# One step of an attention and two expert layers: other order at the start, at the hand-over and in the late steps

## The chip, the cores and the metric

The kernel runs on one core of one Trainium2 chip. The metric is the device time of one execution in microseconds. PE is the matrix engine (TensorE), ACT the scalar engine, DVE the vector engine, POOL GpSimd, and SP the queue that issues most transfers.

## The reference

```python
def _attn_ref(q, k, v, g_norm):                # 4 batches, 8 heads, 576 tokens, 64 wide
    kv = np.einsum('bhsd,bhse->bhde', k, v)
    out = np.einsum('bhsd,bhde->bhse', q, kv)
    rms = np.sqrt(np.mean(out * out, axis=-1, keepdims=True) + 1e-06)
    return (out / rms * g_norm).astype(np.float32)

def _moe_ref(x, domain_probs, w1, w2):         # N=2304, D=512, E=4, F=1024
    p = domain_probs / (domain_probs.sum(-1, keepdims=True) + 1e-09)
    for e in range(E):
        h = np.maximum(x @ w1[e], 0.0)
        out += p[:, e:e + 1] * (h @ w2[e])

def _moe2_ref(x, expert_emb, tau, w1, w2):     # 8 experts, one for each token
    logits = xn @ en.T / tau                   # xn, en: rows divided by their norms
    expert_idx = np.argmax(logits, axis=1)
    gate_w = probs[np.arange(N), expert_idx]   # softmax of the logits
    for e in range(E):
        h = np.maximum(x[mask] @ w1[e], 0.0)
        out[mask] = gate_w[mask, None] * (h @ w2[e])
```

The output of the first becomes x of the second, and its output x of the third.

## The kernel before

The 2304 tokens are 18 tiles of 128, and six units of 384 (three tiles). Each fp32 product of the two expert layers is made of three products of a high part and a low part (split, L60): ACT casts the high part, DVE, or POOL where it is named, subtracts it to get the low part. Instructions run on each engine in the order in which the code issues them, since the schedule is written by hand.

The opening (from L1061): for each of four batches, k and v of two heads give a 64 x 64 product each (kv_unit, L149), copied to a block-diagonal tile kv_bd. For batches 0 and 1 the 576 tokens lie as 72 partitions of 8 rows each (RW = 8), so one unit has 8 steps for two heads, 16 products; for batches 2 and 3 they lie as 128 partitions of 4 rows and a rest of 64 rows, 5 steps, 10 products. In the trace each product of this kind counts as two matrix instructions. Batch 0 uses the tile of the second layer's embeddings (en_b) and the four raw weight buffers; batch 1 uses en_b, two other spare tiles, and for its last pair two raw weight buffers later (last_kv, L1185). The q tiles 0 to 2 are issued by ACT. The first unit's tiles are transposed, multiplied with kv_bd, normalised and transposed again (q_first, x_first, xt_unit); later tiles go through qt_unit, x_unit, x_norm and xt_unit, which are spread over the steps of the expert phases by times in the phase (spread, run_steps, att). An item with time t is issued after the first step whose summed time reaches t. heat() issues filler products.

The first expert layer has phases (p, e, fh): pair of units, expert, half of F. The first four phases run one unit plainly (plain_phase: four products of P1T / 4 each, six second-layer steps), the others a Strassen scheme for two units with 14 + 12 steps (strassen_steps, l2_steps, run_steps at L1240). The raw weight stream has four buffers (issue, take); expert 0's split weights go to DRAM and come back later (hold, fetch).

When a tile of the second layer's input is ready, its logits come by DVE from a reload (logits_v, eight reductions, tiles 0 to 11) or by PE (logits_t, logits_u, tiles 12 to 17). logits_v, route_a and route_b are generators in a list bg; background(n), called after each step, takes up to n pieces from the list and runs what is due at this tick. route_a places the first 12 tiles into NA = 5 jobs of 128 tokens for one expert, route_b the rest into up to 20 jobs. run_steps has the pace n of each step: every second step for the first two pairs of units, every step for the last pair.

The routed jobs (period, full_period, from L1303): period(s) makes the first layer of job s in two halves (m1_unit, line 1267), calls mid1 after each quarter, then the second layer of job s - 1 (m2_unit, line 1289) with mid2 between its quarters, in which the next job's x is transposed and split (ahead_of, tx_unit), and the transposes of h (th_unit). mid1 and mid2 call side(), which issues one weight split from a list (slot_split) and then background(). Job 0 has no second layer beside it; its w2 splits stand in work2, so they are issued after period(0). The placing products are line 513, in invert().

Of the kernel before, what the change touches and what calls it, by code (L numbers as in the profile page):

```python
# [8 lines left out]
F32 = mybir.dt.float32  # L9
# [11 lines left out]
def attn_moe_moe_kernel(ctx: ExitStack, tc: tile.TileContext, q, k, v, g_norm, dprobs, w1, w2, emb, tau, w1b, w2b, out):  # L21
# [98 lines left out]
    RW = 8  # L120
    SR = S // RW

    RL = 2 * RW * DH
    kv_at = {}

    def raw_home():
        return rawp.tile([128, 2 * D], F32, name="raw", tag="raw")

    def kv_homes(b):
        flat = en_b.rearrange("p e n -> p (e n)")  # L130
        part = [flat[:, RL * i:RL * i + RL] for i in range(4)]
        if b == 0:
            homes = part + [raw_home() for _ in range(4)]
        else:
            spare = sum_p.tile([128, 4, 2, 128], F32, name="wsum", tag="wsum").rearrange("p a b c -> p (a b c)")
            homes = [xr[:, 1].rearrange("p c n -> p (c n)"), spare] + part
        for pair in range(len(homes) // 2):
            kv_at[b, pair] = homes[2 * pair:2 * pair + 2]

    def kv_rows(b, pair, o):  # L140
        return kv_at[b, pair][o][0:SR, 0:RL]

    def load_kv_rows(b, pair):
        for o, src in enumerate((k, v)):
            nc.sync.dma_start(
                out=kv_rows(b, pair, o).rearrange("p (h x) -> p h x", h=2),
                in_=src[b, 2 * pair:2 * pair + 2].rearrange("h (p r) d -> p h (r d)", r=RW),
            )

    def kv_unit(b, pair, tag="kv"):  # L150
        ps = psp.tile([128, DH], F32, name="pskv", tag=tag)
        if b < 2:
            kr, vr = (kv_rows(b, pair, o).rearrange("p (h r d) -> p h r d", h=2, d=DH) for o in range(2))
            for c in range(RW):
                for i in range(2):
                    nc.tensor.matmul(out=ps[64 * i:64 * i + 64], lhsT=kr[:, i, c], rhs=vr[:, i, c], start=(c == 0), stop=(c == RW - 1))
        else:
# [11 lines left out]
        if b >= 2:  # L169
            issue()  # L170
# [1228 lines left out]
```

## Time and profile before

| | |
|---|---|
| three runs | 1150.51 us median (1149.87 to 1150.71) |
| the profiled execution | 1150.26 us |
| its span, first to last instruction | 1148.5 us |
| busy PE, DVE, ACT, POOL | 1114.1, 633.1, 486.3, 191.2 us |
| first expert product | 32.95 us after the span's start |
| first Strassen phase | starts near 113 us |
| first product of a routed job | 849.21 us |

The page shows busy time of each engine, the granted clock, transfers and the costliest groups. A timeline row reads: start, duration, engine, line, operation, output<-inputs, count, and in brackets the time for which the engine stood idle before it and what ended that. A busy PE is not PE at full speed: at the lower clock the same product takes longer.

### The profile page before, as it was taken

What the parts mean: (1) busy time and instruction counts of PE and PEld (TensorE: products, weight loads), DVE (VectorE), ACT (ScalarE), POOL (GpSimd) and SP (SyncE); (2) the same over time, 40 slices, a digit from 0 to 9 for tenths busy, and PEclk for the clock granted to TensorE, in tenths of its full rate; (3) what the DMA queues carried; (4) which work ended last, traced back from release to release, by engine and by line L of the source; (5) the groups of instructions that cost most, each with busy time, mean ns of one, the idle gap of its engine ahead of it and who ended that gap; (6) DMA issues with size and microseconds to landing.
All of it is one profiled execution on the core that took longest, in us unless ns stands there. A gap on an engine that the chain in (4) does not pass through costs nothing. (4 is left out here: it accounts for less than half of the span.)

```text
span 1148.5 us, 17340 instructions
## 1 busy us (share of the span) xinstructions
PE 1114.1 (97%) x5982; PEld 974.7 (85%) x5982; DVE 633.1 (55%) x1187; ACT 486.3 (42%) x892; POOL 191.2 (17%) x232
## 2 busy tenths in 40 slices
PE   8899999999999999999999999999997899999997
PEld 8788998888888988899988888999886788888886
DVE  1655664567784556543565684333458674366362
ACT  2534545544454222233333222222456475476462
POOL 1211331223341000100120001000010111211211
PEclk7999999999999999999999999999998899999999
DMA  8664878667777455455464544555454593575571
GB/s 207 180 221 166 311 257 299 236 244 283 284 246 282 166 214 179 170 201 202 174 226 169 220 170 179 200 202 202 171 195 166 184 329 109 172 273 205 168 250 41
DMA packets 87044, 239.87 MB, mean 209 GB/s; under 512 B 17109, under 2 KB 32469, under 8 KB 86816
## 3 DMA queue, kind: packets, MB, share of 16 engines
q1 hardware_dynamic: 76384, 213.44, 52.4%
q0 software_dynamic: 7440, 24.41, 6.2%
q10 hardware_dynamic: 3120, 0.79, 0.4%
q8 instruction: 50, 0.82, 0.3%
q14 instruction: 50, 0.41, 0.1%
HBM read 230.22 MB, written 56.63 MB: 250 GB/s over the span
## 5 line engine op out<-in xcount | busy, mean ns | idle before, releaser
L976 PE MATMUL bank<-w2h,hh 128*128 128x512 f32 x576 | 227.9, 396 | 2.0 <-ACT hh L853 1.9
L976 PE MATMUL bank<-w2l,hh 128*128 128x512 f32 x576 | 225.2, 391 | 0.9 <-DVE w2l L62 0.8
L976 PE MATMUL bank<-w2h,hl 128*128 128x512 f32 x576 | 225.4, 391 | 0.5 <-DVE hl L856 0.5
L881 PE MATMUL bank<-xth,w1h 128*128 128x384 f32 x616 | 160.4, 341 | 4.0 <-ACT s L888 1.4
L881 PE MATMUL bank<-xtl,w1h 128*128 128x384 f32 x616 | 156.8, 335 | 0.0
L881 PE MATMUL bank<-xth,w1l 128*128 128x384 f32 x616 | 156.7, 335 | 0.0
L985 DVE SCALAR_TENSOR_TENSOR acc<-bank,dp,acc 128x512 f32<-128x512 f32 x120 | 89.8, 749 | 110.3 <-PE bank L976 110.1
L976 PEld LDWEIGHTS bank<-w2h,hl 128*128 128x128 f32 x576 | 108.2, 188 | 25.4 <-DVE hl L856 2.4
L976 PEld LDWEIGHTS bank<-w2h,hh 128*128 128x128 f32 x576 | 108.2, 188 | 25.3 <-ACT hh L853 4.0
L976 PEld LDWEIGHTS bank<-w2l,hh 128*128 128x128 f32 x576 | 108.2, 188 | 22.4 <-DVE w2l L62 1.1
L881 PEld LDWEIGHTS bank<-xth,w1h 128*128 128x128 f32 x616 | 109.2, 188 | 9.8 <-ACT s L888 2.2
L881 PEld LDWEIGHTS bank<-xtl,w1h 128*128 128x128 f32 x616 | 111.4, 188 | 0.0
L881 PEld LDWEIGHTS bank<-xth,w1l 128*128 128x128 f32 x616 | 111.3, 188 | 0.0
L62 DVE TENSOR_TENSOR w2l<-raw,w2h 128x1024 fp32r<-128x1024 f32 x64 | 76.5, 1221 | 58.7 <-ACT w2h L61 55.1
L892 POOL TENSOR_TENSOR sv<-sv,s 128x384 f32<-128x384 f32 x44 | 48.8, 1110 | 353.0 <-ACT sv L888 301.3
L888 ACT COPY s<-bank 128x384 f32<-128x384 f32 x88 | 42.3, 481 | 143.7 <-PE bank L881 143.7
L370 DVE CUSTOM_DVE_ANT_0 scr<-row,en_b 128x512 bf16<-128x512 f32 x96 | 68.8, 717 | 17.4 <-DMA row<-x1d 12.6
L1289 PE MATMUL psy<-w2h,hth 128*128 128x512 f32 x176 | 71.6, 407 | 0.4 <-ACT hth L1280 0.4
L1289 PE MATMUL psy<-w2l,hth 128*128 128x512 f32 x176 | 69.5, 395 | 0.0
L1289 PE MATMUL psy<-w2h,htl 128*128 128x512 f32 x176 | 69.2, 393 | 0.0
L61 ACT CAST w2h<-raw 128x1024 fp32r<-128x1024 f32 x64 | 65.5, 1054 | 5.5 <-DMA raw<-in_moe_w_dram 2.1
L62 DVE TENSOR_TENSOR w1l<-raw,w1h 128x256 fp32r<-128x256 f32 (+2 forms) x75 | 55.5, 757 | 19.6 <-ACT w1h L61 19.2
(251 smaller groups left out, 1670.2 us busy)
## 6 DMA issues: line engine op xcount, KB each, us to landing
raw<-in_moe_w_dram SPq DMA_DIRECT2D x224, 512.0 KB
w1h<-held_w SPq DMA_DIRECT2D x28, 896.0 KB
w1l<-held_w SPq DMA_DIRECT2D x28, 896.0 KB
w2h<-held_w SPq DMA_DIRECT2D x34, 512.0 KB
w2l<-held_w SPq DMA_DIRECT2D x34, 512.0 KB
held_w<-w1h SPq DMA_DIRECT2D x16, 896.0 KB
held_w<-w1l SPq DMA_DIRECT2D x16, 896.0 KB
held_w<-w2h SPq DMA_DIRECT2D x16, 512.0 KB
```

The source lines that it names most:

```text
L61: nc.scalar.copy(hi, raw)
L62: (eng or nc.vector).tensor_tensor(out=lo, in0=raw, in1=hi.bitcast(F32), op=ALU.subtract)
L370: nc.vector.tensor_tensor_reduce(out=scr, in0=x, in1=en_b[:, e], scale=1.0, scalar=0.0, op0=ALU.mult, op1=ALU.add, accum_out=lg[:, t, e:e + 1]
L881: nc.tensor.matmul(out=ps, lhsT=wform(wo, b, w)[:, c], rhs=xform(xo, x)[:, c], start=start and n == 0, stop=(n == 5), skip_group_check=True)
L888: nc.scalar.copy(t, src)
L892: (eng or nc.vector).tensor_tensor(out=out, in0=a, in1=b, op=ALU.add)
L976: nc.tensor.matmul(out=ps, lhsT=h_t[o][f][u][:, ns], rhs=w[j][:, a], start=(k == 0 and m == 0), stop=(k == 3 and m == 2))
L985: nc.vector.scalar_tensor_tensor(out=fin, in0=ps, scalar=dp[:, t, e:e + 1], in1=ac, op0=ALU.mult, op1=ALU.add)
L1289: nc.tensor.matmul(out=ps, lhsT=x[:, f], rhs=w[j][:, o], start=(f == 0 and i == 0), stop=(f == NF - 1 and i == 2))
```

## The change

k and v of batches 0 and 1 now also lie as 128 partitions of 4 rows and a rest of 64 rows: batch 0 comes through the raw weight stream, batch 1 into en_b with its rest in a spare tile; the separate last pair is gone. q tiles 0 to 2 are issued by SP behind batch 0. The k/v units of batch 0 share one PSUM buffer and are not mixed with q transposes. The next loads follow as buffers come free. All three direct w1 parts of the first block are split before batch 1's units. In the first two phases the attention steps have times of their own, and w2's splits start at 0 instead of 1. Tile 8's steps are spread over 12 to 28 instead of 17 to 31.1 in their phase. In the last pair of units, experts 0 and 1 have the pace of every second step. The last tile's logits come one tick sooner, and the squares are issued after the copy of the transposes, into another tile. The gate is cut in three: inverse norms ahead of the choice of the expert, the exponential after it, the sum after the places. In period(0) the w2 splits of job 0 stand in the list that mid1 uses.

```diff
-    def load_tail(b):
-        t = kv_p.tile([S - MAIN, 2, H, DH], F32, name="kvtail", tag="tail", bufs=1)
+    def load_tail(b, home=None):
+        t = home if home is not None else kv_p.tile([S - MAIN, 2, H, DH], F32, name="kvtail", tag="tail", bufs=1)
...
     def kv_unit(b, pair, tag="kv"):
+        early = b == 1
+        r = en_b[:, 2 * pair:2 * pair + 2].rearrange("p i n -> p (i n)") if early else take("kv", b, pair)
+        r = r.rearrange("p (i h r d) -> p i h r d", i=2, h=2, d=DH)
+        tl = tail_raw[b]
         ps = psp.tile([128, DH], F32, name="pskv", tag=tag)
-        if b < 2:
-            kr, vr = (kv_rows(b, pair, o).rearrange("p (h r d) -> p h r d", h=2, d=DH) for o in range(2))
-            for c in range(RW):
-                for i in range(2):
-                    nc.tensor.matmul(out=ps[64 * i:64 * i + 64], lhsT=kr[:, i, c], rhs=vr[:, i, c], start=(c == 0), stop=(c == RW - 1))
...
     def logits_t(t, x):
         xx = late["tmp"].tile([128, NC, 128], F32, name="xx", tag="xx")
-        due.append((tick[0] + 2, t, lambda: logits_u(t, xx)))
-        nc.scalar.activation(out=xx.rearrange("p c n -> p (c n)"), in_=x, func=ACTF.Square, accum_out=ssq[:, t:t + 1])
+        due.append((tick[0] + (2 if t < NT - 1 else 1), t, lambda: logits_u(t, xx)))
         ps = psp.tile([128, NC, 128], F32, name="pslt", tag=f"x{t % 2}" if t < NT - 1 else nxt("l2"))
         for c in range(NC):
             nc.tensor.transpose(ps[:, c], x[:, 128 * c:128 * c + 128], ident)
         nc.scalar.copy(xx, ps)
+        sq = late["tmp"].tile([128, R, 128], BF16, name="po", tag="po", bufs=2)
+        nc.scalar.activation(out=sq.rearrange("p r n -> p (r n)"), in_=x, func=ACTF.Square, accum_out=ssq[:, t:t + 1])
...
-    def gates(t0, t1, tag):
...
-        rx = inv_norm(ssq[:, s], [128, T], tag)
-        yield 0
-        tt(l, l, bc(rx, sh, 2), ALU.mult)
-        nc.scalar.activation(out=l, in_=l, func=ACTF.Exp)
-        yield 1
-        nc.vector.tensor_reduce(out=sm, in_=l, axis=AX.X, op=ALU.add)
+    def gate_exp(t0, t1, rx):
+        l = lg[:, t0:t1]
+        tt(l, l, bc(rx, [128, t1 - t0, E2], 2), ALU.mult)
+        nc.scalar.activation(out=l, in_=l, func=ACTF.Exp)
+
+    def gate_sum(t0, t1):
+        s = slice(t0, t1)
+        sm = tmp([128, t1 - t0], "m2")
+        nc.vector.tensor_reduce(out=sm, in_=lg[:, s], axis=AX.X, op=ALU.add)
         ts(sm, sm, 1e-9, ALU.add)
         nc.vector.reciprocal(gate[:, s], sm)
-        yield 0
...
     def route_b():
+        rx = inv_norm(ssq[:, TA:NT], [128, NT - TA], "b")
+        yield 0
         yield from pick(TA, NT)
+        gate_exp(TA, NT, rx)
+        yield 1
         ps, run = ranks(TA, NT)
...
         yield from places(TA, NT, ps, run, tab)
-        yield from gates(TA, NT, "b")
+        gate_sum(TA, NT)
+        yield 0
...
-    stream += raws(0, 0) + raws(0, 1) + raws(0, 0, ("w1",))
+    stream += [("kv", 0, n) for n in range(NP)] + raws(0, 0) + raws(0, 1) + raws(0, 0, ("w1",))
...
     heat(14)
+    for _ in range(RAW):
+        issue()
...
-    kv_homes(0)
-    for p in range(NP):
-        load_kv_rows(0, p)
     for t in range(Q0):
-        load_q(t, nc.scalar, q_first_raw(t))
+        load_q(t, nc.sync, q_first_raw(t))
...
+    for p in range(NP):
+        kv_unit(0, p)
+        heat(2)
...
+    spare = sum_p.tile([128, 4, 2, 128], F32, name="wsum", tag="wsum")
+    issue()
+    load_tail(1, spare.rearrange("p a b c -> p (a b c)")[0:S - MAIN].rearrange("p (i h d) -> p i h d", i=2, d=DH))
+    load_kv1(0)
+    load_kv1(1)
+    issue()
+    load_kv1(2)
+    load_kv1(3)
+    issue()
+    issue()
+    nc.sync.dma_start(out=dp, in_=dprobs.rearrange("(t p) e -> p t e", p=128))
+    for t in range(Q0, Q0 + QB):
+        load_q(t, nc.sync)
...
-    for p in range(NP):
-        kv_unit(0, p, ("kv", "x0", "x1", "l20")[p])
-        if p < 2:
-            heat(2)
-        if p:
-            q_first(p - 1)
...
+    q_first(0)
+    q_first(1)
     for t in range(Q0):
+        if t + 2 < Q0:
+            q_first(t + 2)
         x_first(t)
...
-    w1_direct(0, 0, nc.gpsimd)
+    for part in range(3):
+        w1_direct(0, part, nc.gpsimd)
     for p in range(2):
         kv_unit(1, p, ("kv", "l21")[p])
...
-    for part in range(1, 3):
-        w1_direct(0, part, nc.gpsimd)
+    issue()
...
-    todo = w2_fills(0, 0, 1) + [(-1, lambda part=part: w1_direct(1, part)) for part in range(3)] + [(-1, last_kv)]
-    todo += [(5.5, lambda: kv_unit(1, 2)), (12.0, last_kv_unit), (6.0, norm_probs)]
+    todo = w2_fills(0, 0) + [(-1, f) for f in plain_direct(1)]
+    todo += [(1.5 + 2 * p, lambda p=p: kv_unit(1, p)) for p in range(2, NP)] + [(6.0, norm_probs)]
...
-    plain_phase(0, 0, 0, todo + w1_plain_fills(0, 1) + spread(att([TS]), 9, P2T), [0] * 99)
-    todo = w2_fills(0, 1) + spread(att(range(TS + 1, 2 * TS)), 0, 13)
-    plain_phase(0, 0, 1, todo + [(13.2, lambda: x_split(6, xblock(0, 1))), (14.5, xs_f["b22"])], [0] * 99)
+    plain_phase(0, 0, 0, todo + w1_plain_fills(0, 1) + spread(att([TS]), 4.5, 15.5) + [(16.0, lambda: qt_unit(TS + 1))], [0] * 99)
+    todo = w2_fills(0, 1)
+    for t, at_q, at_x in ((TS + 1, None, 0.1), (TS + 2, 4.0, 6.25)):
+        todo += [(at_x, lambda t=t: x_unit(t)), (at_x + 2.05, lambda t=t: x_norm(t)), (at_x + (6.1, 4.8)[t - TS - 1], lambda t=t: xt_unit(t))]
+        if at_q:
+            todo += [(at_q, lambda t=t: qt_unit(t))]
+    plain_phase(0, 0, 1, todo + [(12.4, lambda: x_split(6, xblock(0, 1))), (13.8, xs_f["b22"])], [0] * 99)
...
-        (0, 2, 0): spread(kv_fills(2), 5.5, 10.2) + spread(att([8]), 17, S2T),
+        (0, 2, 0): spread(kv_fills(2), 5.5, 10.2) + spread(att([8]), 12, 28),
...
-        run_steps(steps, todo, [i % 2 if p < UNITS // 2 - 1 else 1 for i in range(len(steps))])
+        run_steps(steps, todo, [i % 2 if p < UNITS // 2 - 1 or e < 2 else 1 for i in range(len(steps))])
...
     def full_period(s):
-        work1 = [lambda n=n: slot_split("w1", s + 1, [n]) for n in range(4 if 0 < s < NS - 1 else 0)]
         work2 = [lambda n=n: slot_split("w2", s, [n]) for n in range(4)]
+        work1 = [lambda n=n: slot_split("w1", s + 1, [n]) for n in range(4 if s + 1 < NS else 0)]
+        if s == 0:
+            work1, work2 = work2, []
```

## Rows read from the trace of the kernel before

**Rows 1.** The page's first part: busy time of each engine, share, instructions.

```profile
PE 1114.1 (97%) x5982; PEld 974.7 (85%) x5982; DVE 633.1 (55%) x1187; ACT 486.3 (42%) x892; POOL 191.2 (17%) x232
```

**Rows 2.** Busy time by stretch, 10 to 20 us; last three: granted clock, DMA share, GB/s.

```profile
10.00:15.00 5.00, 3.23 (x38) 3.15 (x39) 0.00 (x0) 0.41 (x2) 0.00 (x0) 0.57 0.81 209
15.00:20.00 5.00, 5.00 (x66) 4.22 (x66) 0.69 (x1) 1.00 (x3) 0.00 (x0) 0.50 0.55 144
```

**Rows 3.** The timeline of the opening, matrix engine alone.

```profile
11.77 1.98 PE L156 MATMUL pskv<-en_b 72*64 72x64 f32 x32 [2.48 <-DMA en_b<-in_v_dram]
...
21.45 4.22 PE L214 MATMUL psx<-kvbd,acc 128*128 128x128 f32 x24
...
32.95 0.93 PE L869 MATMUL bank<-xth,w1h 128*128 128x384 f32 x4 [1.44 <-ACT w1h L61]
```

**Rows 4.** The DMA view: 0 to 35 us in total, 0 to 5 (two queues), 24 to 35.

```profile
DMA packets 9623, 7.17 MB, mean 205 GB/s; under 512 B 6069, under 2 KB 7093, under 8 KB 9621
...
q1 hardware_dynamic: 231, 0.45, 34.9%
q10 hardware_dynamic: 1019, 0.26, 28.0%
...
q1 hardware_dynamic: 4222, 2.66, 89.9%
```

**Rows 5.** The timeline of the first plain phases, matrix engine alone.

```profile
39.36 1.15 PE L156 MATMUL pskv<-en_b 72*64 72x64 f32 x32
...
45.57 0.50 PE L976 MATMUL bank<-w2l,hh 128*128 128x512 f32 x1 [0.76 <-DVE w2l L62]
...
56.41 0.66 PE L259 MATMUL psxt<-ident,xs 128*128 128x128 f32 x4 [1.29 <-DVE xs L236]
...
56.82 0.95 PE L869 MATMUL bank<-xth,w1h 128*128 128x384 f32 x4
...
75.14 0.63 PE L259 MATMUL psxt<-ident,xs 128*128 128x128 f32 x4 [1.41 <-DVE xs L236]
...
79.72 0.87 PE L869 MATMUL bank<-xth,w1h 128*128 128x384 f32 x4
...
96.27 0.87 PE L869 MATMUL bank<-xth,w1h 128*128 128x384 f32 x4
```

**Rows 6.** The timeline at the end of phase (0, 2, 0).

```profile
215.93 0.63 PE L259 MATMUL psxt<-ident,xs 128*128 128x128 f32 x4 [1.00 <-DVE xs L236]
```

**Rows 7.** The timeline of phase (2, 0, 0), the last unit's first.

```profile
585.80 0.62 PE L881 MATMUL bank<-xth,w1h 128*128 128x384 f32 x2 [0.57 <-DVE acc L985]
...
605.77 0.50 PE L976 MATMUL bank<-w2h,hh 128*128 128x512 f32 x1 [1.08 <-ACT hh L853]
```

**Rows 8.** The page's costliest groups: busy and mean ns; idle before and releaser.

```profile
L370 DVE CUSTOM_DVE_ANT_0 scr<-row,en_b 128x512 bf16<-128x512 f32 x96 | 68.8, 717 | 17.4 <-DMA row<-x1d 12.6
```

**Rows 9.** The timeline of the hand-over to the routed jobs.

```profile
855.88 0.21 DVE L393 TENSOR_TENSOR lg<-lg,rt 128x48 f32<-128x48 f32 x1
...
858.69 0.48 PE L1267 MATMUL psm<-w1h,xgh 128*128 128x512 f32 x1
...
859.09 3.92 ACT L61 CAST w2h<-raw 128x1024 fp32r<-128x1024 f32 x4
...
860.21 4.63 DVE L62 TENSOR_TENSOR w2l<-raw,w2h 128x1024 fp32r<-128x1024 f32 x4
...
868.17 1.28 ACT L431 ACT_TABLE_LOAD   x1 [0.45 <-DVE iny L252]
...
871.48 1.23 DVE L62 TENSOR_TENSOR w2l<-raw,w2h 128x1024 fp32r<-128x1024 f32 x1 [1.96 <-ACT w2h L61]
...
877.58 0.79 PE L1267 MATMUL psm<-xth,xgl 128*128 128x512 f32 x1 [3.91 <-DVE xgl L393]
...
893.17 0.75 PE L513 MATMUL psi<-rhs,po 128*128 128x100 bf16 x4 [4.04 <-DVE po L397]
```

**Rows 10.** Busy time by stretch, as in rows 2, behind job 2's wait.

```profile
875.00:880.00 5.00, 2.42 (x6) 1.94 (x7) 4.62 (x21) 2.27 (x4) 2.58 (x2) 0.50 0.66 238
```

More of the change, by code (lines that the diff above doesn't have):

```diff
@@ L118, in load_tail @@
         tail_raw[b] = t
[L120 to L148, printed above, removed]
     def kv_unit(b, pair, tag="kv"):
+        early = b == 1
+        r = en_b[:, 2 * pair:2 * pair + 2].rearrange("p i n -> p (i n)") if early else take("kv", b, pair)
@@ L151, in kv_unit @@
+        r = r.rearrange("p (i h r d) -> p i h r d", i=2, h=2, d=DH)
+        tl = tail_raw[b]
         ps = psp.tile([128, DH], F32, name="pskv", tag=tag)
-        if b < 2:
-            kr, vr = (kv_rows(b, pair, o).rearrange("p (h r d) -> p h r d", h=2, d=DH) for o in range(2))
-            for c in range(RW):
-                for i in range(2):
-                    nc.tensor.matmul(out=ps[64 * i:64 * i + 64], lhsT=kr[:, i, c], rhs=vr[:, i, c], start=(c == 0), stop=(c == RW - 1))
-        else:
-            r = take("kv", b, pair).rearrange("p (i h r d) -> p i h r d", i=2, h=2, d=DH)
-            tl = tail_raw[b]
-            for c in range(RC):
-                for i in range(2):
-                    nc.tensor.matmul(out=ps[64 * i:64 * i + 64], lhsT=r[:, 0, i, c], rhs=r[:, 1, i, c], start=(c == 0), stop=False)
+        for c in range(RC):
@@ L163, in kv_unit @@
             for i in range(2):
-                hd = 2 * pair + i
-                nc.tensor.matmul(out=ps[64 * i:64 * i + 64], lhsT=tl[:, 0, hd], rhs=tl[:, 1, hd], start=False, stop=True)
+                nc.tensor.matmul(out=ps[64 * i:64 * i + 64], lhsT=r[:, 0, i, c], rhs=r[:, 1, i, c], start=(c == 0), stop=False)
+        for i in range(2):
+            hd = 2 * pair + i
+            nc.tensor.matmul(out=ps[64 * i:64 * i + 64], lhsT=tl[:, 0, hd], rhs=tl[:, 1, hd], start=False, stop=True)
         for i in range(2):
@@ L168, in kv_unit @@
             nc.scalar.copy(kv_bd[b % 2][sl, pair, sl], ps[sl])
-        if b >= 2:
+        if b > 1:
             issue()
@@ L527, in route_a @@
     def route_a():
+        rx = inv_norm(ssq[:, 0:TA], [128, TA], "a")
         yield from pick(0, TA)
+        gate_exp(0, TA, rx)
+        yield 1
         ps, run = ranks(0, TA)
@@ L546, in route_a @@
         nc.vector.scalar_tensor_tensor(out=sl[:, 0:TA], in0=lim[:, 0:TA], scalar=-64.0, in1=jobs[:, 0:TA], op0=ALU.mult, op1=ALU.add)
-        yield from gates(0, TA, "a")
+        gate_sum(0, TA)
+        yield 0
         yield from invert(TA, 0, NA, sl[:, 0:TA])
@@ L1087, in x_first @@
         nc.vector.tensor_reduce(out=ms[:, t], in_=x_s[t], axis=AX.X, op=ALU.add)
-    for p in range(NP):
-        kv_unit(0, p, ("kv", "x0", "x1", "l20")[p])
-        if p < 2:
-            heat(2)
-        if p:
-            q_first(p - 1)
-    kv_homes(1)
-    issue()
-    for p in range(2):
-        load_kv_rows(1, p)
-    for _ in range(RAW - 1):
-        issue()
-    load_kv_rows(1, 2)
-    nc.sync.dma_start(out=dp, in_=dprobs.rearrange("(t p) e -> p t e", p=128))
-    for t in range(Q0, Q0 + QB):
-        load_q(t, nc.sync)
+    q_first(0)
+    q_first(1)
     for t in range(Q0):
+        if t + 2 < Q0:
+            q_first(t + 2)
         x_first(t)
```

15 lines of the change are left out of this document (4 added, 11 removed).

## The prediction

> **What bounds the kernel now.** I read the page first: the matrix engine is busy 97% of the span [rows 1], so a change can win only where it stands or runs at its lower clock. The list of waits of that engine, then the timeline around each wait, give the places. Four are touched by the change.
>
> The opening comes first. From 11.77, when pair 1 of k and v lands, the engine runs one serial chain at the lower of its two clocks: granted clock 0.57, then 0.50, that is 1.2 GHz, in 10 to 20 us [rows 2]. The products with q take 4.22 us from 21.45, and the first expert product starts at 32.95 [rows 3].
>
> Then the two first plain phases, 32.95 to 56.82 and 56.82 to 79.72, last 23.87 and 22.90, where the third one, with no attention work in it, lasts 16.55 [rows 5]. Their stalls: the engine waits 0.76 for a low part of w2, and 1.29 and 1.41 for normalised x [rows 5]; the starts of the products around these two show some 0.15 more lost at each, 1.45 and 1.57.
>
> Third, single waits later: 1.00 for x of tile 8 [rows 6], and five in the first phase of the last unit, from 585.80 on, 3.03 us together, of which rows 7 show the first and the longest. VectorE causes them: it has 717 ns logits reductions of the previous unit queued between the sums and low parts that products wait for [rows 7, 8].
>
> Fourth, the hand-over to the routed jobs: job 2 waits 3.91 for the low part of its x, and the placing products wait 4.04 for a comparison [rows 9]; the clock is granted at 0.50 after the first [rows 10]. Both releasers are VectorE, which works without a real gap from 871.48 to 893.
>
> **Opening.** Bytes stay nearly the same: batch 0 is 2.36 MB of k and v and 0.79 MB of q. Before, pieces of 2 KB take 0.349 x 16 x 5 us / 231 = 121 ns each and pieces of 256 B take 0.280 x 16 x 5 / 1019 = 22 ns [rows 4]. After, the main part comes in 1 KB pieces; no row isolates these, so the bounds are half a 2 KB piece, 60 ns, and the mean piece of 24 to 35 us, 0.899 x 16 x 11 / 4222 = 37 ns [rows 4]. That mean holds many smaller ones, so I take 58. The two rests of 64 rows come in 1024 pieces of 256 B: 1024 x 22 / 16 = 1.4 us a batch, added to the path. Sum to the third q tile: (1024 x 22 + 2048 x 58 + 3072 x 22) / 16 = 13 us, so it lands near 15.5 when the stream starts at 1.75.
>
> The Trainium skill, "DMA: Bandwidth & Descriptors", Specifications, asks for at least 512 bytes a transfer and so speaks against the new rests. The row agrees in kind: 256 B in 22 ns is 11.6 GB/s for one engine against 17 with 2 KB pieces. By either the rests cost a microsecond or two, not the opening.
>
> All of q now goes out on SP behind ten k and v transfers, no longer on ACT; that delays q and brings k and v forward, and the products need k and v first. Pairs land about 6, 8, 10 and 11.5, each followed by 20 instead of 32 short instructions and filler, so the engine stands for less than a microsecond at a time where it stood 2.48 [rows 3]. Four units in one PSUM buffer add a wait for two ACT copies each; filler covers it. The q transposes and products then end near 20.5 (full clock) to 22 (half), against 25.67. From there the chain of statistics, norm and transposes is as before, 7.3 us, less about 0.4, because the casts of two w1 parts are issued ahead of it. First product: 27.8, against 32.95: **5.1 gained**, between 3 (half clock and k/v of batch 1 landing late) and 6.5.
>
> SP holds more behind waits: each weight load waits for a k/v unit of batch 0, and batch 1, dp and the q tiles 3 and 4 stand behind them. The stream to q tile 3 is (45 + 238 + 90 + 59 + 62 + 40) us of engine time (rests, pairs, q, w1, w2, dp) / 16 = 33.4, so q tile 3 lands near 36; its transposes now come at 5.9 instead of 10 in the phase, that is at 34.5. **1.0 lost.** Cover gone, everything behind it on PE moves with that landing.
>
> **First two phases.** Two k/v units of 1.15 [rows 5] shrink to 20/32: 0.8. The low part of w2 is issued one product earlier, and then is ready before its use: the 0.76, and some 0.5 around it, since the high part, for which the product before it waits, comes equally early (estimate); 1.3. Tile 3's norm moves from after the fourth second-layer step to after the third and is first in VectorE's order there, so 1.45 goes. First phase: 3.5. In the second phase the last norm and its transposes stay two steps apart, with the w2 split on ACT and VectorE between, so most of the 1.57 stays late: 0.9. **4.4 gained**, between 2 and 6. Together with the opening: 5.1 + 4.4 - 1.0 = **8.5**.
>
> **Tile 8 and half pace.** Tile 8's norm and transposes, 4 units of phase time apart instead of 3.5 and well before the phase's end: **1.1 gained**, 0.3 at least. Half pace in the first four phases of the last unit puts out one logits step per two steps, so that a product's sums meet one reduction of 0.72 in VectorE's queue instead of two. Of the 3.03 (3.8 with 0.15 to recover for each wait) between none and all can go; I take 2.2, and 0.4 in the next phases; the logits and the first routing then reach into the third expert at full pace, counted through its steps: the gather comes near step 9 of its second half, over a phase before its user, so no new wait. **2.6 gained**, 1 to 3.7.
>
> **Hand-over.** The four w2 splits of job 0 (3.92 on ACT, 4.63 on VectorE [rows 9]) move from behind job 0's first layer to between its products. Before, they hid behind job 1's first layer, which ran from 858.69 with no wait. Now ACT has the second split behind the first half's ReLU (854), VectorE's low part follows at 855.2, and the last logits copy, though issued a step sooner, stands behind it in VectorE's queue: about 856.5, where the first routing instruction now starts at 855.88 [rows 9]. Then come some 14 short routing instructions of about 0.21 (as the first in [rows 9]) with the square root now between them, two more low parts and job 1's own low part: 855.2 + 3.6 + 0.3 + 3.4 + 0.7 = 863.2. So job 1's third product waits until 863.4, where it ran two products of 0.23 behind 858.69, at 859.2: 4.2 later, plus about 1.7 if the clock falls as it did to 0.50 behind the 3.91 wait [rows 9, 10].
>
> What is given back: ACT no longer holds job 1's w2 splits behind the gate's square root and exponential. The first low part follows the first layer by about 1.8 us; before, it came at 871.48, some 7 after its end at 858.69 + 24 x 0.233 = 864.3. So it starts at 870.6 to 872.4. From there to the placing product VectorE's list is the same 21.7 us. That is 0.9 sooner to 0.9 later than 893.17; with three pauses in six microseconds I expect the lower clock: **1.0 lost** with the tail, between 1.5 gained and 2.5 lost. The 3.91 wait shrinks to about 0.6, but moves: ahead of job 1, and into the 4.04 wait, which grows.
>
> The square root loads its table on ACT between the splits, 1.28 by the row [rows 9], already in the walk. The Trainium skill, "ScalarE: Activation LUTs", What ACT_TABLE_LOAD costs, adds a drain of 1.38; here exp starts right after its load, so the row decides; with the drain the hand-over would lose 2.4.
>
> The squares that now follow the copy, and land in another tile, take one wait off ACT in steps where PE waits for neither: nothing, and nothing if that cover goes, as the logits product comes two steps later. Steady jobs are untouched.
>
> **Sum.** The profiled execution took 1150.26 (median 1150.51). 1150.3 - 8.5 - 1.1 - 2.6 + 1.0 = **1139.1**.
>
> **Rivals.** (a) VectorE is relieved as the move intends: the splits fill its gaps at 849 to 858, job 1 does not wait, and its low part follows 864.3 by 1.8 instead of 7: 5.3 earlier, 1139.1 - 1.0 - 5.3 = 1132.8. For it: that stretch lies ahead of all routing work [rows 9]. Against: job 1's x stands behind the splits in both queues. (b) The single stream binds: at 205 GB/s, the mean of the first 35 us [rows 4], 7.9 MB put q tile 3 at 40.3; 35.2 us of unstalled work follow to the third phase, which starts at 75.5, not 71.2: 1143.4. For it: 209 and 144 GB/s in 10 to 20 us [rows 2]; against: the gaps there are waits of issues, and 24 to 35 us moved 2.66 MB, 242 GB/s [rows 4]. (c) Slower: the same stream, slowed to the 144 GB/s of 15 to 20 us by small pieces and by weight loads that hold SP. Then q tile 3 lands at 56.6, the third phase starts at 91.8 against 79.72, and with the other parts' 2.7 the time is 1159.7. It decides below 174 GB/s; the change turns slower by over 0.2% below 165. (d) The logits step does not come sooner, since its copy waits in VectorE's queue; this is in the forecast.
>
> **Chances.** Forecast 0.61, (a) 0.12, (b) 0.16, (c) 0.07, and 0.04 that gains and losses meet within 0.2% (2.3 us, about what a measurement of this kernel tells from no change). Faster: 0.89; same 0.04; slower 0.07. Range 1132 to 1146: it takes in (a) and (b) with their bounds, leaving out (c) and the ends where all terms go one way.
>
> **What would show it.** Right: the first expert product near 28, the first wait for normalised x gone and the third phase near 71; of the five waits in the first phase of the last unit only the first left; a wait of some 4 us ahead of job 1's first layer, and the placing product at nearly the same distance from job 0's start. Wrong: q transposes waiting for a transfer beyond 38; job 1 starting as early as before, and no wait for job 2's x; waits for VectorE in the third expert's phases of the last unit.

## The result and the profile after

The changed kernel takes 1139.28 us (median of 6 runs, 1138.08 to 1142.47) against 1150.19 for the kernel before beside it: a ratio of 0.9912, 95% interval 0.9898 to 0.9926. Its profiled execution took 1139.33, with a span of 1137.5; before they were 1150.26 and 1148.5. The forecast of 1139.1 was met almost exactly, and for the wrong reasons: three of its terms were far off and cancelled each other.

The first part of the page shows as little as before [rows 1]: busy time, share and instructions of each engine.

```profile
span 1137.5 us, 17164 instructions
PE 1106.6 (97%) x5894; PEld 970.7 (85%) x5894; DVE 629.6 (55%) x1187; ACT 484.9 (43%) x892; POOL 190.1 (17%) x232
```

What tells is a comparison of starts. I took from both timelines of the matrix engine where each stage begins, and subtracted:

| stage | starts before | starts after | won up to its start | won in the stage ahead of it | forecast for that |
|---|---|---|---|---|---|
| first expert product | 32.95 | 26.27 | 6.68 | 6.68 | 5.1 |
| second plain phase | 56.82 | 47.74 | 9.08 | 2.40 | 3.5, less 1.0 (q tile 3) |
| third plain phase | 79.72 | 75.45 | 4.27 | -4.81 | 0.9 |
| end of phase (0, 2, 0) | 217.79 | 212.29 | 5.50 | 1.23 | 1.1 |
| phase (1, 3, 1) | 554.05 | 548.81 | 5.24 | -0.26 | 0 |
| phase (2, 3, 0) | 779.83 | 767.37 | 12.46 | 7.22 | 2.6 |
| phase (2, 3, 1) | 810.77 | 798.31 | 12.46 | 0 | 0 |
| job 0 | 849.21 | 838.06 | 11.15 | -1.31 | 0 |
| job 2's second layer, beside job 3 | 905.08 | 894.11 | 10.97 | -0.18 | -1.0 |

Behind that the jobs run as before.

**Opening.** The timeline of the matrix engine, and busy time by stretch (columns as in [rows 2]: the last three are granted clock, DMA share and GB/s):

```profile
7.46 0.69 PE L128 MATMUL pskv<-raw 128*64 128x64 f32 x16 [1.17 <-DMA raw<-in_v_dram]
...
15.92 0.66 PE L163 MATMUL psq<-ident,xr 128*128 128x128 f32 x4 [0.92 <-DMA xr<-in_q_dram]
...
16.41 2.84 PE L180 MATMUL psx<-kvbd,acc 128*128 128x128 f32 x24
...
26.27 0.94 PE L841 MATMUL bank<-xth,w1h 128*128 128x384 f32 x4 [1.42 <-DVE xtl L233]
```

```profile
10.00:15.00 5.00, 4.99 (x64) 3.95 (x64) 0.61 (x1) 1.24 (x6) 0.00 (x0) 1.00 1.14 260
15.00:20.00 5.00, 4.08 (x37) 4.09 (x38) 2.23 (x5) 2.38 (x4) 0.00 (x0) 1.00 1.07 267
```

The longest wait for data is 1.17 where it was 2.48 [rows 3], and the clock is granted at 1.00 where it was 0.57 and 0.50 [rows 2].

**Second plain phase.** The matrix engine's timeline, then VectorE's and ScalarE's, and the stretch behind the longest wait:

```profile
45.50 0.66 PE L225 MATMUL psxt<-ident,xs 128*128 128x128 f32 x4 [0.32 <-DVE xs L202]
...
60.62 1.09 PE L225 MATMUL psxt<-ident,xs 128*128 128x128 f32 x4 [4.22 <-DVE xs L202]
...
75.45 0.87 PE L841 MATMUL bank<-xth,w1h 128*128 128x384 f32 x4
```

```profile
57.24 1.23 DVE L62 TENSOR_TENSOR w2l<-raw,w2h 128x1024 fp32r<-128x1024 f32 x1 [3.76 <-DMA held_w<-w2l]
...
58.85 0.19 DVE L217 RECIPROCAL ry<-rs 128x8 f32<-128x8 f32 x1
...
59.78 0.69 DVE L202 TENSOR_TENSOR xs<-psx,rs 128x512 f32<-128x512 f32 x1
```

```profile
55.95 1.05 ACT L61 CAST w2h<-raw 128x1024 fp32r<-128x1024 f32 x1 [2.67 <-DMA held_w<-w2h]
```

```profile
60.00:65.00 5.00, 4.38 (x18) 4.41 (x19) 1.62 (x3) 1.48 (x3) 2.83 (x4) 0.50 0.27 94
```

Of the waits in [rows 5], 1.29 has become 0.32 and the other two are gone, but a new one of 4.22 stands ahead of tile 4's transposes. Read backwards: the transposes need tile 4's norm (59.78), that stands in VectorE's order behind the low part of w2 (57.24), and that waits 3.76 for the transfer that stores the old w2 block, which is still in the buffer that it fills. Behind the wait the granted clock is 0.50 from 60 to 65 us and 0.90 in the next five, where it was 1.00 in the kernel before, so the phase loses more than the wait alone.

**Last unit.** In (2, 0, 0) no wait is left of those of [rows 7]. **(2, 3, 1)** has waits that were shorter or absent:

```profile
822.35 0.66 PE L346 MATMUL pslt<-ident,fin 128*128 128x128 f32 x4 [0.60 <-DVE fin L957]
...
831.67 0.66 PE L346 MATMUL pslt<-ident,fin 128*128 128x128 f32 x4 [0.65 <-DVE fin L957]
```

**Hand-over.** The matrix engine's waits, as in [rows 9], and VectorE's queue ahead of the last of them:

```profile
851.30 0.80 PE L1240 MATMUL psm<-w1h,xgh 128*128 128x512 f32 x1 [3.62 <-ACT xgh L1123]
...
866.75 0.50 PE L1240 MATMUL psm<-xth,xgl 128*128 128x512 f32 x1 [0.39 <-DVE xgl L360]
...
878.88 0.75 PE L476 MATMUL psi<-rhs,po 128*128 128x100 bf16 x4 [5.38 <-DVE po L364]
```

```profile
875.10 2.95 DVE L62 TENSOR_TENSOR w1l<-raw,w1h 128x1024 fp32r<-128x1024 f32 x3
877.97 0.68 DVE L62 TENSOR_TENSOR xtl<-raw,xth 128x512 fp32r<-128x512 f32 x1
878.57 1.62 DVE L364 TENSOR_SCALAR po<-lane_b,pos 128x128 bf16<-128x128 bf16 x8
```

The 3.91 shrank to 0.39, a new wait of 3.62 stands ahead of job 1, and the 4.04 grew to 5.38.

### The profile page after: what moved, and what is told of

Read it like the earlier page. It is cut to its first block, busy times and chain, and to the rows that moved or that the text cites. A ratio compares the mean times of both kernels' runs of the same rounds, so it can differ in the third digit from the quotient of the medians.

```text
span 1137.5 us, 17164 instructions
## 1 busy us (share of the span) xinstructions
PE 1106.6 (97%) x5894; PEld 970.7 (85%) x5894; DVE 629.6 (55%) x1187; ACT 484.9 (43%) x892; POOL 190.1 (17%) x232
```

## Experiments

Unless it says otherwise, an edit is made to the changed kernel, and a time is the median of its runs beside runs of the kernel before (1149.2 to 1149.4 in all of these comparisons, 1150.19 beside the changed kernel). Intervals of the ratios are 0.0010 to 0.0020 to either side, 1.1 to 2.3 us, so differences of a microsecond are read from phases of the traces. Where the granted clock is 1.00 these repeat closely: phase (2, 3, 1) takes 39.75 to 39.77 in the changed kernel and in the six below that leave it as it is there.

### The second plain phase

```
-        todo += [(at_x + 2.05, lambda t=t: x_norm(t)), ...
+        todo += [(at_x + (1.95 if t == TS + 1 else 2.05), lambda t=t: x_norm(t)), ...
```

> The changed kernel with one edit: in the second plain phase tile 4's norm is emitted just ahead of the first w2 split instead of just behind it. Theory A (the new 4.22 us wait of the transposes at 60.62 is VectorE's order: the norm's reciprocal stands behind a w2 split that itself waits 3.76 us for the store of the old w2 block): the wait at 60.62 is gone, the second phase takes about 23.5 us instead of 27.7, the clock stays at full level behind it, and the program gains about 4, to near 1135. Something of the wait may stay one step on, at tile 5's scores, since ScalarE's copy of its q transposes stands behind the w2 cast (2.67 us wait) in the same way: then 1 us less. Rival B (the transposes stand too early in TensorE's own order, ahead of the fourth product, and whatever they wait for is late): the phase stays above 26 us and the program within 1.5 us of 1139.3.

It took 1136.47, ratio 0.9889 (0.9875 to 0.9903). The wait of 4.22 is gone, the phase takes 24.93 us where it took 27.71. In the matrix engine's timeline three smaller waits stand in its place:

```profile
58.07 0.66 PE L225 MATMUL psxt<-ident,xs 128*128 128x128 f32 x4 [1.33 <-ACT qT L169]
...
63.99 0.50 PE L948 MATMUL bank<-w2l,hh 128*128 128x512 f32 x1 [0.64 <-DVE w2l L62]
...
67.02 0.66 PE L225 MATMUL psxt<-ident,xs 128*128 128x128 f32 x4 [1.37 <-DVE xs L202]
```

Theory A holds: nothing but VectorE's order was changed. The first of the three is ScalarE's queue, as expected: the w2 cast waits there for the same store, with tile 5's q copy behind it. The granted clock stays at 1.00 here, so part of the 2.78 that the phase gains is the clock; the runs don't part it from the wait. The phase is 1.4 longer than expected. A kernel below, which moves the w2 splits themselves one step later, brings it to 22.87.

### Half pace alone

To the kernel before:

```
-        run_steps(steps, todo, [i % 2 if p < UNITS // 2 - 1 else 1 for i in range(len(steps))])
+        run_steps(steps, todo, [i % 2 if p < UNITS // 2 - 1 or e < 2 else 1 for i in range(len(steps))])
```

> The kernel before with one edit: the half pace of the background work also in the first two experts of the last pair of units, as in the changed kernel. The forecast's price for this part was 2.6 us (1147.6). Theory A (read from the trace of the changed kernel): 4.0 in the phase that starts at 585.8, about 3.6 in the two that follow the next, 1.9 given back two phases later, in all about 7.2 with the phases between: near 1143. Theory B (the 7.2 comes partly from another edit, the later order of the steps in the phases before it): no more than 4 us, 1146 or above. In both the phase from 810.77 to job 0's first layer keeps its 38.4 us, if the 1.3 lost there in the changed kernel belong to the order of square and copy.

1144.52, ratio 0.9957 (0.9944 to 0.9969): 4.8 us by the medians, 3.6 to 6.4 by the interval. By phases of the two profiled executions it is 6.6: 0.8 in (1, 3, 1), 4.0 in (2, 0, 0), 0.8, 1.7 and 1.8 in the three phases behind it, then 1.0 and 1.5 lost in (2, 2, 0) and (2, 2, 1), to which the first routing has moved. The changed kernel shows the same pattern, 0.8, 4.0, 0.8, 1.7 and 1.8 won and 0.8 and 1.1 lost. The price belongs to this one line, and it is above the forecast's bound of 3.7 by the phases, and at or above it by the medians. (2, 3, 1) keeps 38.4.

### The order of square and copy

```
         ps = psp.tile([128, NC, 128], F32, name="pslt", ...)
+        if t < NT - 1:
+            nc.scalar.activation(out=sq..., in_=x, func=ACTF.Square, accum_out=ssq[:, t:t + 1])
         for c in range(NC): ...transpose...
         nc.scalar.copy(xx, ps)
-        nc.scalar.activation(out=sq..., in_=x, func=ACTF.Square, accum_out=ssq[:, t:t + 1])
+        if t == NT - 1: ...the same
```

> The changed kernel with the square of a late tile's logits ahead of its transposes and their copy again, on ScalarE, for all tiles but the last, which keeps the changed order. Theory A (ScalarE idles while the transposes run, so the square behind the copy puts off the two casts that follow by 0.56 us per tile, the split on VectorE with them, and the next tile's sum behind that): the phase ahead of job 0's first layer takes 38.4 us instead of 39.75, the waits of 0.60 and 0.65 us of the transposes go, and the program gains about 1.3, to near 1138. Rival B (the 1.3 us come from routing that the half pace put off into this phase): 39.7 us stay, no change.

1137.59, ratio 0.9897 (0.9883 to 0.9911). Phase (2, 3, 1) takes 38.10 instead of 39.75: 1.65, and the waits of 0.60 and 0.65 are gone. It takes 38.10 also in the three kernels below that keep this edit. ScalarE's timeline of the changed kernel shows where they come from:

```profile
818.23 0.59 ACT L347 COPY xx<-pslt 128x512 f32<-128x512 f32 x1 [1.72 <-PE pslt L346]
818.72 0.63 ACT L349 ACTIVATE po<-fin 128x512 bf16<-128x512 f32 x1
...
819.34 1.99 ACT L61 CAST xth<-raw 128x1024 fp32r<-128x1024 f32 x2
```

ScalarE stands while the transposes run, and the square that could fill that time comes behind the copy. The casts start later by it, VectorE's low parts after them, and the next tile's sum behind those. Theory A holds.

### The hand-over

Four edits, each alone. Job 0's splits behind its products again:

```
-        work1 = [... for n in range(4 if s + 1 < NS else 0)]
-        if s == 0:
-            work1, work2 = work2, []
+        work1 = [... for n in range(4 if 0 < s < NS - 1 else 0)]
```

> The changed kernel with the hand-over's split order of the kernel before: job 0's four w2 splits behind its products, none of job 1's w1 splits displaced. The forecast put the move at 1.0 lost (between 1.5 gained and 2.5 lost), so this kernel near 1138.3. Theory A (VectorE's queue ahead of job 1's operand is what the move lengthens): job 1's first layer starts 9.5 us behind job 0's instead of 13.24, job 3's 49.3 instead of 50.4, gain about 1. Rival B (the splits must be done somewhere before job 0's second layer, and between the products they hide best): job 1 starts earlier but job 0's second layer waits as long, job 3's distance 50.4 or more, and the program is not faster than 1139.3.

1139.67, ratio 0.9920 (0.9905 to 0.9934): no difference. The waits of the matrix engine:

```profile
848.80 0.50 PE L1240 MATMUL psm<-w1h,xgh 128*128 128x512 f32 x1 [1.37 <-ACT xgh L1123]
...
867.38 0.64 PE L1240 MATMUL psm<-xth,xgl 128*128 128x512 f32 x1 [4.55 <-DVE xgl L360]
...
879.51 0.75 PE L476 MATMUL psi<-rhs,po 128*128 128x100 bf16 x4 [3.84 <-DVE po L364]
```

Rival B: job 1 starts 10.62 behind job 0 instead of 13.24, and job 2's x waits 4.55. The move only carries waiting time from one place to another.

The second routing's root and exponential behind its places again:

```
     def route_b():
-        rx = inv_norm(ssq[:, TA:NT], [128, NT - TA], "b")
-        yield 0
         yield from pick(TA, NT)
-        gate_exp(TA, NT, rx)
-        yield 1
...
+        rx = inv_norm(ssq[:, TA:NT], [128, NT - TA], "b")
+        yield 0
+        gate_exp(TA, NT, rx)
+        yield 1
         gate_sum(TA, NT)
```

> The changed kernel with the square root and exponential of the last six tiles' gates behind their places again, as in the kernel before. Theory A (job 1's x high part stands on ScalarE behind that exponential, which waits 1.33 us for VectorE's low parts): job 1's first product starts about 2 us sooner than 13.24 us behind job 0's, with a second wait of some 2 us then for the low part; the sum at job 1's second layer is sooner by no more than 0.7, and the table loads, now later, cost as much: within 1 us of 1139.3. Rival B (the place of the exponential is what lost the hand-over): 1.5 us or more faster, job 1's first layer waits under 1 us in all.

1137.26, ratio 0.9891 (0.9875 to 0.9906). The matrix engine's waits:

```profile
846.70 0.42 PE L415 MATMUL psr<-oh,ones 128*128 128x48 f32 x2 [0.98 <-DVE oh L360]
...
850.42 0.50 PE L1240 MATMUL psm<-w1h,xgl 128*128 128x512 f32 x1 [1.21 <-DVE xgl L360]
...
864.28 0.50 PE L1240 MATMUL psm<-xth,xgl 128*128 128x512 f32 x1 [1.14 <-DVE xgl L360]
...
878.07 0.76 PE L476 MATMUL psi<-rhs,po 128*128 128x100 bf16 x4 [5.28 <-DVE po L364]
```

One wait of 3.62 became two of 0.98 and 1.21. Job 1's second layer comes 2.2 sooner behind job 0's first (job 0's own 3.0), where theory A allowed 0.7, and the program is 2.0 us faster by the medians, nearer to rival B (the intervals of the two ratios overlap a little). The sum of the waits falls by 1.0 only; the rest is the clock, as shown below the last table.

The placing products three steps later:

```
-        yield 1
+        yield 1 if k0 == 0 else 4
         ps = psp.tile([128, 5, n], F32, name="psi", tag="kv")
```

> The changed kernel with one edit: the second routing's comparisons and placing products are put out three background steps later (a rest of four steps instead of one ahead of them), so they stand in TensorE's order behind job 1's second layer instead of after its first quarter. Theory A (the hand-over brings nothing because TensorE reaches the placing product's place in its order 5.38 us ahead of VectorE, which has four w1 low parts queued before the comparisons, and waits there with work ready behind): the wait of 5.38 shrinks to under 1.5, job 3's first layer starts 46 to 48 us behind job 0's instead of 50.4, the clock falls for a shorter time, and the program ends 3 to 4 us earlier, near 1135.5. Rival B (VectorE's list as a whole sets the hand-over's end, and the waits only move): the wait comes back at job 3's operands or at the gather for job 5, the distance stays near 50, and the program stays within 1 us of 1139.3.

1135.37, ratio 0.9876 (0.9860 to 0.9892): as theory A had it. The wait is 2.18 instead of 5.38 (under 1.5 was expected), and job 3 starts at 43.84 behind job 0, even earlier than expected, since some placing products now follow that start. Its timeline:

```profile
879.44 0.70 PE L476 MATMUL psi<-rhs,po 128*128 128x100 bf16 x4 [2.18 <-DVE po L364]
...
881.16 0.78 PE L1240 MATMUL psm<-w1h,xgh 128*128 128x512 f32 x1
```

### The opening

First q on ScalarE's queue:

```
     for t in range(Q0):
-        load_q(t, nc.sync, q_first_raw(t))
+        load_q(t, nc.scalar, q_first_raw(t))
```

> The changed kernel with the first three q tiles issued by ScalarE again instead of by SyncE behind batch 0's k and v. Theory A (the opening gains 6.7 us because k and v come in larger pieces, in order, undisturbed, so that TensorE never stands long and its clock is granted at 1.00 in 5 to 20 us): with q beside them the pairs land up to 2.3 us later (0.79 MB at the 340 GB/s of that time), TensorE stands longer between pairs, first product near 28. Rival B (the larger pieces alone do it, the same bytes arrive in either order): first product within 0.5 us of 26.3 and the program within 1 us of 1139.3.

1145.10, ratio 0.9951 (0.9935 to 0.9967). The opening is back where it was, although in 10 to 20 us more bytes come than in either kernel. Timeline and stretches:

```profile
9.39 1.12 PE L128 MATMUL pskv<-raw 128*64 128x64 f32 x16 [2.52 <-DMA raw<-in_v_dram]
...
32.43 0.76 PE L841 MATMUL bank<-xth,w1h 128*128 128x384 f32 x3 [1.41 <-DVE xtl L233]
```

```profile
10.00:15.00 5.00, 5.00 (x49) 4.08 (x47) 0.00 (x0) 0.83 (x4) 0.00 (x0) 0.50 1.11 372
15.00:20.00 5.00, 5.00 (x48) 4.31 (x47) 0.00 (x0) 0.83 (x4) 0.00 (x0) 0.50 1.11 347
```

The first pair lands 1.9 us later, as in theory A, but the first product comes 6.2 later, where theory A gave 1.7. The difference is the clock at 0.50: the engine never waits for data again, it works at half rate until past 20 us. The Trainium skill, "DMA: Bandwidth & Descriptors", Issuing engines are not separate DMA queues, says that transfers of several issuing engines interleave on the same 16 DMA engines and only save the time of issuing. The trace agrees: q beside k and v takes 34.0% of the engines' time in the first 12 us, and the first pair pays for it.

Then the same kernel with the wait filled:

```
-    heat(14)
+    heat(21)
```

> The changed kernel with q on ScalarE's queue as in the run before of that kind (first product 32.43 there), and 21 filler products instead of 14 at the start, 2.49 us more, over the 2.52 us in which TensorE waited for the first pair until 9.39. Theory A (q on its own queue cost 6.2 us not through bytes but through the clock: the wait of 2.52 took the grant to 0.50 from 10 to 21 us, where the changed kernel's wait of 1.17 left it at 1.00): the grant stays at 1.00 and the first product comes at 27 to 28.5, 2 us behind the changed kernel's 26.3 at most for the later pair. Rival B (the later arrival of the pairs is what costs): first product above 31.

1140.17, ratio 0.9927 (0.9907 to 0.9947). The wait is 1.38, the clock stays at 1.00, the first product comes at 27.22, 5.2 us sooner than without these seven filler products. Not every run follows: of six runs each, one without the seven products took 1140.91 (the others 1143.85 to 1145.72), and one with them 1146.65 (the others 1139.22 to 1141.15). Neither left a trace, so why stays open. Timeline and stretches again:

```profile
9.82 0.69 PE L128 MATMUL pskv<-raw 128*64 128x64 f32 x16 [1.38 <-DMA raw<-in_v_dram]
...
27.22 0.93 PE L841 MATMUL bank<-xth,w1h 128*128 128x384 f32 x4 [1.42 <-DVE xtl L233]
```

```profile
10.00:15.00 5.00, 5.00 (x88) 4.16 (x85) 0.00 (x0) 1.24 (x6) 0.00 (x0) 1.00 1.11 372
15.00:20.00 5.00, 5.00 (x48) 4.72 (x45) 2.09 (x4) 2.19 (x5) 0.00 (x0) 1.00 1.11 350
```

And the kernel before with its wait filled:

```
         if p < 2:
-            heat(2)
+            heat((9, 2)[p])
```

> The kernel before with one edit: nine filler products instead of two behind the first k and v unit, 2.49 us more at the 0.355 us of one, so that TensorE works through the 2.48 us in which it waited for pair 1. Theory A (the opening is bound by the clock: that wait takes the grant to 0.57 and 0.50 for 10 to 25 us, and the serial chain runs at half rate): the grant stays at 1.00, the chain of units, transposes and products with q ends 4 to 5 us sooner than 25.5, the first expert product comes near 28.5, and what remains of the changed kernel's 6.7 is what a later wait for pairs 2 and 3 costs. Rival B (the arrival of pairs 2 and 3 and of q, in 2 KB pieces beside q, is the bound, and the half clock only fills the time): first product within 1 us of 32.95.

Here theory A fails: 1151.41, ratio 1.0023 (1.0013 to 1.0033), first product at 32.03, only 0.92 sooner. The matrix engine's timeline, and one stretch:

```profile
11.39 1.15 PE L156 MATMUL pskv<-en_b 72*64 72x64 f32 x32 [0.74 <-DMA en_b<-in_v_dram]
...
14.40 1.15 PE L156 MATMUL pskv<-raw 72*64 72x64 f32 x32 [0.79 <-DMA raw<-in_v_dram]
...
17.50 1.97 PE L156 MATMUL pskv<-raw 72*64 72x64 f32 x32 [1.36 <-DMA raw<-in_v_dram]
```

```profile
15.00:20.00 5.00, 3.64 (x59) 3.25 (x56) 0.00 (x0) 1.41 (x5) 0.00 (x0) 0.68 0.84 242
```

At full clock the engine meets the later pairs, 14.40 and 17.50, and after the third wait the clock falls all the same. In the changed kernel the last pair's unit runs at 12.33. So the opening's gain takes both: pairs of which the last comes five microseconds sooner, and no waits among them that bring the clock down. What the old arrival would allow at a clock of 1.00 throughout was not measured, since the clock fell here too. Of the 0.92, 0.6 is lost in the second plain phase and 1.4 more in the fourth, where the matrix engine waits 0.67 and 0.66 for reloaded w2 blocks; why it ends slower than the kernel before was not followed further.

### Together

The square's order, the placing products three steps later, and in the second plain phase:

```
-    todo = w2_fills(0, 1)
+    todo = [(4.1, lambda: fill_w2(0, 2)), (6.3, lambda: fill_w2(0, 3))]
```

> The changed kernel with three edits together: in the second plain phase both w2 splits one step later, behind tile 4's norm and tile 5's q copy; the square of the late logits ahead of the copy, but for the last tile; the placing products three steps later. Theory: the three prices add, as each stands at its own place: 2.0 kept from the norm's place and about 1 more for the later splits, 1.3 for the squares, 3 to 4 for the placing products: 1131 to 1133. Rival: what is won early is given back at the hand-over, where VectorE's list sets the end: 1135 or above.

1128.93, ratio 0.9820 (0.9807 to 0.9834), better than expected: 4.84 from the second plain phase, 1.65 from (2, 3, 1), about 4.6 from the hand-over. With the later exponential as a fourth:

> The three edits of the kernel that took 1128.9, and with them the square root and exponential of the last gates behind their places again, which alone took the changed kernel from 1139.3 to 1137.3. Theory A (the waits ahead of job 1 and the one ahead of the placing products are two separate places): job 1's wait of 3.62 falls to about 1.2, 1.7 of it stay to the end: near 1127.2. Rival B (VectorE's list up to the comparisons sets the time once the placing products stand later): the time won ahead of job 1 comes back in the wait of 2.18 ahead of the placing products: within 0.5 of 1128.9.

1127.07, ratio 0.9808 (0.9795 to 0.9821): the time that theory A gave, but not by its sum of waits. Job 1's waits fall as expected, yet others grow, the one ahead of the placing products from 2.18 to 2.64, and the sum goes from 6.3 to 6.0 only; the rest is the clock (table below). And with the placing products one step later again (a rest of 5):

> The kernel with four edits (1127.07, the placing products three steps later than in the changed kernel) with the placing products one step later again. Theory A (they still come 2.64 us too early for VectorE, which has four w1 low parts of 3.63 us to finish first): the wait of 2.64 falls under 1 and the program gains 1 to 1.7, near 1125.7. Rival B (what is put off must then be drained ahead of job 2's second layer, where each group of comparisons of 0.74 us stands alone in the path): the wait moves there, and the time stays within 0.7 of 1127.1 or is longer.

1126.48, ratio 0.9807 (0.9791 to 0.9823). The wait of 2.64 became two of 1.46 and 0.71; the trace gains 0.4, which the runs can't tell from nothing. Theory A's gain is not there; the time lies within rival B's 0.7.

One table shows the hand-over in nine of these kernels. The length is from job 0's first layer to job 2's second layer, which stands beside job 3; the waits are the sum of the matrix engine's list of waits there, the clock the mean granted one:

| kernel | length | waits | clock |
|---|---|---|---|
| before | 55.87 | 9.5 | 0.88 |
| changed | 56.05 | 9.6 | 0.91 |
| norm ahead of the split | 54.60 | 9.3 | 0.94 |
| square first | 55.27 | 9.4 | 0.91 |
| job 0's splits behind | 56.02 | 9.8 | 0.91 |
| exponential later | 54.36 | 8.6 | 0.94 |
| placing products later | 51.66 | 6.4 | 0.93 |
| three places | 51.49 | 6.3 | 0.93 |
| four places | 48.74 | 6.0 | 1.00 |

The third row has the hand-over of the second, instruction for instruction, so 1.4 us between kernels there mean nothing by themselves. The last two rows differ by 0.3 in waits and by 2.75 in length: the clock is 1.00 throughout in the last. This goes with the wait ahead of job 1, since it repeats: in all seven traces that have the wait of 3.62 there the granted clock falls behind it, in the changed kernel to 0.80 and 0.85 from 10 to 20 us behind job 0's start, and in the three edited kernels with the later exponential it is 1.00 in that stretch. The first half of it in the changed kernel:

```profile
848.06:853.06 5.00, 1.76 (x4) 1.43 (x5) 4.22 (x7) 2.83 (x5) 0.00 (x0) 0.80 0.66 191
```

The length of one wait does not tell whether the clock falls: the last row has one of 2.64 at 1.00, and the wait of 2.52 in the opening was followed by 0.50.

## Why the prediction came out right, point by point

**Opening: mechanism right, size too small, by 1.6, and tile 3's 1.0 not paid.** The step that was mis-sized is what follows the third q tile. Its landing was forecast near 15.5, and the transposes start on it at 15.92. From there the forecast gave the matrix engine until 20.5 at full clock or 22 at half to end the products with q, without a row for it; they end at 19.25. The chain behind them took 7.0 for 6.9. The first two pairs came later than forecast, at 7.46 and 9.29 for 6 and 8, and that cost only the short waits at full clock.

The piece of 1 KB at 58 ns was mis-sized too. In the first 12 us of the changed kernel the queue moves 4582 packets in 77.6% of 16 engines' time, 149 us; 2534 of these have 256 B and take 56 at 22 ns [rows 4], which leaves 46 ns for each of the 2048 pieces of 1 KB, an estimate. Over the 4096 pieces of two batches and 16 engines that is 3.1 us, and q tile 3's transposes start at 33.58 without a wait, where its landing was forecast near 36. Why the third q tile did not come sooner by its part of that was not followed. The Trainium skill, "DMA: Bandwidth & Descriptors", Specifications, which spoke against the 256 B rests, is not contradicted; here the rests were simply cheaper than what the 1 KB pieces won: by these estimates a batch takes 7.3 us of 16 engines' time, for 8.7 in pieces of 2 KB at 121 ns.

What I did not see is how much hung on the clock: the forecast let it be full or half and gave 1.5 us for that; the runs with and without filler put 5.2 on it.

**First phase: right in kind, 2.40 for 3.5.** The 0.76 is gone. Of 1.29, 0.32 stays, tile 4's q transposes (0.35 by their place in the order) moved into this phase, which I had not booked, and the two k/v units won 0.4 and not 0.8: a unit with its fewer products, over 128 partitions, takes 0.88 (32.70 to 33.58) where it took 1.08 (39.36 to 40.44).

**Second phase: the step that failed.** I wrote that "the last norm and its transposes stay two steps apart, with the w2 split on ACT and VectorE between", and looked at tile 5 alone. Tile 4's norm is the one that the split stands ahead of, and the split was given no wait of its own. That wait could be read before; it is in VectorE's timeline of the kernel before, where the norm also follows it, but late enough that no transposes stood waiting:

```profile
63.55 1.23 DVE L62 TENSOR_TENSOR w2l<-raw,w2h 128x1024 fp32r<-128x1024 f32 x1 [3.25 <-DMA held_w<-w2l]
...
67.22 0.69 DVE L236 TENSOR_TENSOR xs<-psx,rs 128x512 f32<-128x512 f32 x1
```

A wait of an engine that had cost nothing became the matrix engine's longest of these phases when dependent work moved behind it, and it took the clock down with it: 0.9 forecast, 4.81 lost. So the third phase starts at 75.45, not near 71 as the forecast's sign had it. Rival (b) had 75.5, but by a late q tile 3, which nothing waited for.

**Tile 8: right**, 1.23 for 1.1 (read from the trace, not tried alone).

**Half pace: mechanism right, size off by more than two.** The term took 2.2, of 3.0 to 3.8, in one phase and 0.4 in all others. All 4.0 of (2, 0, 0) went, the first of the five waits too, which the forecast left, and the three phases behind it gave 4.3 more. I had not priced what the first routing costs the phases in which it runs: 1.7 and 1.8 before, 0.8 and 1.1 in the two phases of the third expert, to which the slower pace puts it. Why it costs less there was not tried.

**Squares behind the copy: booked at nothing, cost 1.3 to 1.65.** I looked at whether the matrix engine waits for the square, not at what is queued behind it on ScalarE.

**Hand-over: nearly right in sum, wrong in its steps.** The wait ahead of job 1 (3.62 for "some 4 us") and the shrinking of the 3.91 came in size. The walk had job 1's third product wait for VectorE's low part; it is the first that waits, for the high part on ScalarE, behind the exponential as much as behind the splits: without the move of the splits the wait is 1.37, with the later exponential 0.98 and 1.21. The placing product does not stay at its distance from job 0: it comes 3.1 sooner (40.82 for 43.96). That brought nothing, as it stands earlier in the matrix engine's order as well, with four w1 low parts ahead of it on VectorE. Rival (a), the relief of VectorE, is out: undoing the move of the splits changes nothing. Rivals (b) and (c) fell with the stream, which moved 260 to 267 GB/s in 10 to 20 us.

Of the forecast's total, then, the opening and half pace were 1.6 + 1.0 + 4.6 too low, first and second phase, squares and drift 1.1 + 5.7 + 1.3 + 0.3 too high, and the hand-over came 0.8 better. The sum was luck of signs.

## What to carry to other kernels

Before work is moved on an engine's queue, read the waits of the instructions that it will stand behind, also those that cost nothing so far: a split that waits 3 us for a store is harmless until something urgent follows it. Where a stage has several waits whose sum hardly changes under reordering (8.6 to 9.8 in the first six rows of the table), look at the order of the engine that waits: putting its products where their operands are due won what moving the operands' producers did not. And fill a wait that takes the clock down: what follows it at half clock can cost more than the wait. Short waits in its place are no cure by themselves: 0.74, 0.79 and 1.36 in a row were followed by 0.68.

## What the runs showed of the hardware

- Seven filler products (2.5 us) in front of the first pair were worth 5.2 us: with a wait of 2.52 the granted clock was 0.50 from 10 to 20 us (1.2 of 2.4 GHz) although the engine was busy all of that time; with 1.38 it was 1.00.
- Equal instructions can differ in time by the clock: the hand-over of two kernels with the same instructions there, and waits within 0.3 us, took 56.05 and 54.60, at a mean granted clock of 0.91 and 0.94.
- A granted clock of 0.50 outlasts the wait ahead of it: behind the wait of 4.22 that ended at 60.62 it was 0.50 in the stretch to 65, although the matrix engine was busy for 4.38 of the 5 us from 60.
- Pieces of 1 KB cost an engine some 46 ns, an estimate from one queue's share, against 22 for 256 B and 121 for 2 KB [rows 4], estimates of the same kind.
